# Row-tiled pairs for half of the Q projection, and another order of the K stage, in a block of linear attention plus GEGLU on one Trainium2 core

## Chip, cores and metric

The kernel runs on one core of one Trainium2 chip. The metric is the device time of one execution in microseconds (us). Lower is better. All matrices are bf16, with sums in f32.

The engines are named as in the profile: PE is TensorE's matmul, PEld its weight load, DVE is VectorE, ACT is ScalarE, POOL is GpSimd, SP is SyncE (here it only issues transfers and hands on signals). Each engine works through its own instructions in the order in which the program issues them.

## What is computed

```python
def _A_ref(x, wqkv, wo):                      # x: 1 x 2048 x 576, 32 heads of 18
    q, k, v = split_heads(x @ wqkv)
    phi = lambda t: jnp.where(t > 0, t + 1, jnp.exp(t)) + 1e-6
    pq, pk = phi(q), phi(k)
    kv = jnp.einsum("bhsd,bhse->bhde", pk, v)
    z = jnp.einsum("bhsd->bhd", pk)
    num = jnp.einsum("bhqd,bhde->bhqe", pq, kv)
    den = jnp.einsum("bhqd,bhd->bhq", pq, z)[..., None] + 1e-6
    return merge_heads(num / den) @ wo

def _B_ref(x, w_gate, w_up, w_down):          # inner size 4608
    return (_gelu(x @ w_gate) * (x @ w_up)) @ w_down

xn = _layernorm(A_x)
return A_x + _A_ref(xn, A_wqkv, A_wo) + _B_ref(xn, B_w_gate, B_w_up, B_w_down)
```

## The kernel before

The 2048 tokens are 16 tiles of 128 (`NS`) or 4 slices of 512 (`NSC`). The 576 features are 4 full tiles of 128 rows and one of 64; in the normalized input `xn` the last 64 columns are stored twice, so its fifth tile also has 128 rows. The 32 heads are 5 chunks (`NCH`): four of 7 heads (126 rows) and one of 4 (72 rows). PSUM is one tensor `ps_all` of 8 banks of 512 f32.

**K stage** (16 token tiles). For a tile n: DVE takes statistics of two halves and aggregates them (`ln_half`, L200 and L202); ACT makes 1/sqrt by Ln and Exp (`ln_rstd`, L206, L207); DVE normalizes (`ln_norm`, L210); POOL stores the last 64 columns a second time (`ln_dup`, L216); PE transposes five tiles into bank 7 (`transposes`, L222); ACT copies them to `xnT` (`tp_copy`, L226); PE makes K in two halves of 288 columns, banks 5 and 6 (`k_half`, L234); ACT reads each half with relu (L251), DVE with max (L255), ACT takes one exp over both (L262), and POOL adds the two into `pk` (L266). DVE's read of a bank waits for ACT's read of it.

V is never made. In its place PE sums the Gram matrix of `xn` and `pk` over the tokens (`g_accumulate`, L281): part `G_A` in the K stage in banks 0 to 4, two tiles behind K (`GLAG`), ten matmuls a tile; the remainder `G_B`, two matmuls a tile, later in banks 0 and 1, once `G_A` has been copied to `g_sb` (`g_copy`, L428).

The order of the K stage is a timetable: `STEPS` (L387) gives each step of a tile a time for tiles 0 to 4 and then a step of 2.5 (`TILE`) per tile; all steps of all tiles are sorted by that time and issued in this order. All transfers up to the first four gate/up blocks are issued ahead of it (L413 to L420).

**Q part** (20 units: 4 slices by 5 chunks, `q_unit`). A unit is five matmuls with 512 columns (L306), then phi: mostly relu and exp on ACT, max on DVE and an add on POOL; every third unit one exp on ACT and two steps on DVE. The intermediate tiles are `phi_e` (three buffers) and `phi_a` (two). Units 0 and 1 are in the timetable, units 2 to 19 in the loop at L431, which also carries: the last two tiles of `G_A`, the copies of `g_sb`, the z product (`z_stage`, L343, masked into `zrep`), the remainder `G_B` in units 6 to 13, the denominators of slice 0 in units 13 to 17 (`den_mm`, L366, evicted by ACT), and the product of `wv` and the Gram matrix (`kv_stage`, L354, masked into `kvT`) at unit 17.

**Gate/up and down**, once for each slice. `gu_pair` takes blocks of two units; a unit is a gate and an up product of 128 inner columns. These run in row tiles: the array is used as two halves of 64 rows that work at the same time, LO and HI, on different banks (`_Unit`). In the first half `p1` the gate product takes the LO rows and the up product the HI rows, ten matmuls; in the second half `p2` they change sides, eight matmuls, and a signal that goes from PE to SP and back (`turn`, L488) keeps one bank from being written by both. The second halves follow the first halves of the next unit. Then comes gelu on ACT (L522) and the product on DVE (L523), while the denominators of slice 0 are inverted on DVE and multiplied on POOL (`den_norm`). The down product (L550) and the attention's output (L555) follow. The first load of `w_down` (L461) waits until the buffers of the attention part have been read.

Of the kernel before, what the change touches and what calls it, by code (L numbers as in the profile page):

```python
# [15 lines left out]
P = 128  # L16
# [23 lines left out]
GLAG = 2  # L40
XW = 642
# [14 lines left out]
def kernel(  # L56
# [45 lines left out]

    def load_w(which):
        c = slice(which * D, (which + 1) * D)
        nc.sync.dma_start(wqkv_sb[:, 0:4, c], A_wqkv[0:512, c].rearrange("(kt p) c -> p kt c", p=P))
        nc.sync.dma_start(wqkv_sb[0:HP, 4, c], A_wqkv[512:576, c])

# [89 lines left out]
    def ln_half(n, a_):  # L197
        if a_ == 0:
            stats_t[n] = asmall.tile([P, 2, nc.vector.BN_STATS_DIM], F32, name="stats")
        nc.vector.bn_stats(out=stats_t[n][:, a_, :], in_=x_sb[:, n, a_ * HALF:(a_ + 1) * HALF])  # L200
        if a_ == 1:
            nc.vector.bn_aggr(out=mv[:, n, :], in_=stats_t.pop(n)[:])  # L202

    def ln_rstd(n):
        r = rstd[:, n:n + 1]
        nc.scalar.activation(out=r, in_=mv[:, n, 1:2], func=ACT.Ln, bias=eps_ln[:], scale=1.0)  # L206
        nc.scalar.activation(out=r, in_=r, func=ACT.Exp, scale=-0.5)  # L207

    def ln_norm(n):
        nc.vector.tensor_scalar(  # L210
            out=xn[:, n, 0:D], in0=x_sb[:, n, :], scalar1=mv[:, n, 0:1], scalar2=rstd[:, n:n + 1],
            op0=ALU.subtract, op1=ALU.mult,
        )

    def ln_dup(n):
        (nc.gpsimd if n else nc.vector).tensor_copy(out=xn[:, n, D:640], in_=xn[:, n, 512:D])  # L216
# [7 lines left out]
    def tp_copy(n):  # L224
        copy = acopy if n else vcopy
        copy(out=xnT[:, :, n * P:(n + 1) * P], in_=tp_bank[:, 0:KT, :])  # L226
# [20 lines left out]
    def k_relu(n, hf):  # L247
        if hf == 0:
            k_ea[n] = phi_tiles()
        hs = slice(hf * HALF, (hf + 1) * HALF)  # L250
        nc.scalar.activation(out=k_ea[n][0][:, hs], in_=ps_all[:, k_bank(n, hf), :HALF], func=ACT.Relu, scale=-1.0)  # L251

    def k_max(n, hf):
        hs = slice(hf * HALF, (hf + 1) * HALF)
        nc.vector.tensor_scalar(  # L255
            out=k_ea[n][1][:, hs], in0=ps_all[:, k_bank(n, hf), :HALF],
            scalar1=0.0, scalar2=EPS_ATT, op0=ALU.max, op1=ALU.add,
        )

    def k_exp(n):  # L260
        e = k_ea[n][0]
        nc.scalar.activation(out=e[:], in_=e[:], func=ACT.Exp, scale=-1.0)  # L262

    def k_add(n):
        e, a = k_ea.pop(n)
        nc.gpsimd.tensor_tensor(out=pk[:, n, :], in0=e[:], in1=a[:], op=ALU.add)  # L266
# [10 lines left out]
    def g_accumulate(n, pieces):  # L277
# [7 lines left out]

    vcopy, acopy = nc.vector.tensor_copy, nc.scalar.copy

    G_COPIES = {
        4: [(0, G_A, 0, acopy), (0, G_A, 1, vcopy), (2, G_A, 0, acopy), (2, G_A, 1, vcopy)],
# [4 lines left out]
    }  # L294

# [3 lines left out]
    def q_unit(i):  # L299
# [3 lines left out]
        cs = slice(sc * SC, (sc + 1) * SC)  # L303
        ps = ps_all[:rows, q_banks.next(), :]
        for kt in range(KT):
            nc.tensor.matmul(  # L306
                ps, lhsT=wqkv_sb[:, kt, q0:q0 + rows], rhs=xnT[:, kt, cs],
                start=(kt == 0), stop=(kt == KT - 1),
            )
        e, a = phi_tiles()  # L310
# [63 lines left out]
    def den_norm(sc, c, q, pieces):  # L374
# [8 lines left out]

    TILE = 2.5
    STEPS = [  # L387
        (lambda n: ln_half(n, 0), [3.02, 3.99, 6.44, 7.41, 9.44]),
        (lambda n: ln_half(n, 1), [3.51, 4.48, 6.93, 7.90, 9.93]),
        (ln_rstd, [4.14, 5.11, 7.56, 10.12, 11.84]),  # L390
        (ln_norm, [4.96, 5.69, 8.38, 10.77, 12.80]),
        (ln_dup, [5.43, 6.16, 8.85, 11.24, 13.27]),
        (transposes, [5.66, 6.57, 9.14, 11.53, 13.62]),
        (tp_copy, [6.07, 6.98, 9.56, 12.27, 14.12]),
        (lambda n: k_half(n, 0), [6.86, 8.09, 10.30, 13.01, 15.56]),
        (lambda n: k_half(n, 1), [7.47, 9.43, 10.91, 13.91, 16.46]),
        (lambda n: k_relu(n, 0), [7.99, 9.28, 11.56, 13.84, 16.55]),
        (lambda n: k_relu(n, 1), [8.27, 10.55, 12.83, 15.11, 17.39]),
        (lambda n: k_max(n, 0), [8.72, 10.41, 12.44, 14.61, 17.27]),
        (lambda n: k_max(n, 1), [9.08, 11.11, 13.28, 15.60, 17.84]),  # L400
        (k_exp, [8.73, 11.12, 13.29, 15.61, 18.10]),
        (k_add, [9.59, 11.73, 14.01, 16.29, 19.88]),
    ]
    G_AT = [11.82, 14.53, 17.07, 19.62, 22.16]

    def at(times, n):
        return times[n] if n < len(times) else times[-1] + TILE * (n - len(times) + 1)

    todo = [(at(times, n), step, n) for n in range(NS) for step, times in STEPS]
    todo += [(at(G_AT, n), lambda n: g_accumulate(n, G_A), n) for n in range(NS - GLAG)]  # L410

    todo += [(at(STEPS[7][1], NS - 1) - 0.01, q_unit, 0), (at(G_AT, NS - GLAG) - 0.01, q_unit, 1)]
    load_x(8, 4)  # L413
    load_x(12, 4)
    load_w(0)
    load_w(2)
    load_wo()
    for i in range(NWBUF):
        load_gu(i, 0)
        load_gu(i, 1)  # L420
    for _, step, n in sorted(todo, key=lambda x: x[0]):
        step(n)
# [8 lines left out]
    for i in range(2, NSC * NCH):  # L431
# [3 lines left out]
        if 3 <= i < 3 + GLAG:  # L435
            g_accumulate(NS - GLAG + i - 3, G_A)
        for kt, pieces, part, copy in G_COPIES.get(i, ()):
            g_copy(kt, pieces, part, copy)
        if i == 10:
            z_stage()  # L440
        if 6 <= i < 14:
            for n in (2 * (i - 6), 2 * (i - 6) + 1):
                g_accumulate(n, G_B)
        if 13 <= i < 13 + NCH:
            den_mm(0, i - 13, q_banks.next())
        if i == 17:
            kv_stage()
# [16 lines left out]

    LO, HI = slice(0, HP), slice(HP, P)
    SYNC = mybir.DependencyInfo(mybir.DependencyClass.Sync, mybir.DependencyReason.DATA)
    banks = _Ring(list(range(8)))  # L470

    class _Unit:


        def __init__(self, outs, lhs, rhs):
            self.outs, self.lhs, self.rhs = outs, lhs, rhs

        def mm(self, i, rows, kt, start, stop):
            return nc.tensor.matmul(  # L479
                self.outs[i], lhsT=self.lhs(i, rows, kt), rhs=self.rhs(i, rows, kt),  # L480
                start=start, stop=stop, skip_group_check=True,
            )

        def p1(self):
            for kt in (4, 0, 1, 2, 3):
                self.mm(0, LO, kt, kt == 4, False)
                last = self.mm(1, HI, kt, kt == 4, False)
            self.turn = nc.sync.nop()  # L488
            tc.add_manual_dep(self.turn.ins, last.ins.name, SYNC, reason="the row tiles take turns on a bank")

        def p2(self):
            for kt in range(4):
                m = self.mm(1, LO, kt, False, kt == 3)
                if kt == 0:
                    tc.add_manual_dep(m.ins, self.turn.ins.name, SYNC, reason="the bank's other row tile has written")
                self.mm(0, HI, kt, False, kt == 3)
# [28 lines left out]
    m_banks = _Ring(list(range(2, 8)))  # L525
# [85 lines left out]
```

## Time and profile before

| | us |
|---|---|
| median of 5 runs | 531.38 |
| lowest, highest | 530.52, 531.57 |
| the profiled execution | 531.57 |
| its span | 529.8 |
| first transposes on PE | 5.50 |
| first Gram step on PE | 12.79 |
| first Q unit on PE | 43.96 |
| first gate/up matmul | 76.94 |
| first gelu | 80.18 |

The span runs from the first to the last recorded instruction; a time of an execution holds 1.77 us more. Times in the timeline are from the start of the span. The shares of busy time are averages over stages: up to 44 us the K stage, to 77 us the Q part, then four rounds of gate/up and down. The granted clock of TensorE is full in all 40 slices.

In a line of the timeline stand the start, the length, the engine, the line of the code, the operation, what it writes and reads, and how many instructions were merged; in brackets the idle time before and what ended it. Matmuls are pipelined: one that follows another starts before the other's recorded end.

### The profile page before, as it was taken

Reading aid. Unit: us, or ns where it says so; the run is one execution under the profiler, and the core shown is the slowest. Engines: PE = TensorE matmul, PEld = TensorE weight load, DVE = VectorE, ACT = ScalarE, POOL = GpSimd, SP = SyncE. Lnnn points to the kernel's source line nnn. Section 1 sums busy time; section 2 is a strip of 40 time slices with the busy share of each in tenths; the row PEclk is TensorE's granted clock in tenths of the full one; section 3 lists DMA queues with packets and bytes.
Section 4 is the critical chain, followed back from the end, with each engine's and each line's share of the span. In section 5 each row is a group of like instructions: output and inputs, shape, how many; then the busy total and the mean of one; then the engine's idle time right before and its main releaser. Section 6 shows DMA issues by size and latency. Waiting matters only on the chain.

```text
span 529.8 us, 10752 instructions
## 1 busy us (share of the span) xinstructions
PE 521.6 (98%) x4532; PEld 311.6 (59%) x4532; DVE 246.9 (47%) x408; ACT 153.7 (29%) x296; POOL 70.3 (13%) x83
## 2 busy tenths in 40 slices
PE   7999999999999999999999999999999999999997
PEld 6887664444477754444477744444677544445775
DVE  7884767773348513333368233333585143333101
ACT  6997693323230013323200022323100132322000
POOL 3666552110002100000012000000021000000000
PEclk9999999999999999999999999999999999999999
DMA  8910006999510025555400055555100355540000
GB/s 269 263 30 1 1 2 198 263 265 260 149 31 20 16 80 152 148 149 157 136 12 12 12 151 162 148 157 156 47 22 12 95 145 158 155 135 1 12 12 22
DMA packets 98810, 55.85 MB, mean 105 GB/s; under 512 B 5322, under 2 KB 98378, under 8 KB 98762
## 3 DMA queue, kind: packets, MB, share of 16 engines
q1 hardware_dynamic: 98762, 55.17, 36.2%
q8 instruction: 35, 0.57, 0.4%
q14 instruction: 13, 0.11, 0.1%
HBM read 52.79 MB, written 2.36 MB: 104 GB/s over the span
## 4 chain that ended last, share of the span: by engine, by line
PE 93%; SPq 3%; DMA 1%; DVE 1%; issue 1%; POOL 0%; ACT 0%; DVEq 0%; POOLq 0%; ACTq 0%
PE ps_all L479 50%; PE ps_all L550 27%; PE ps_all L306 4%; PE ps_all L555 4%; PE ps_all L281 3%; PE ps_all L234 3%; DMA x_sb<-in_A_x_dram 1%; SPq L165 1%; PE ps_all L366 1%; PE ps_all L222 1%; SPq L167 1%; SPq L168 1%; SPq L92 0%; DVE phi_a L255 0%; DVE stats L200 0%
## 5 line engine op out<-in xcount | busy, mean ns | idle before, releaser
L479 PE MATMUL ps_all<-xnT,wu 64*128 64x512 bf16 x1152 | 273.2, 376 | 1.1 <-SPq L488 0.5
L479 PE MATMUL ps_all<-xnT,wg 64*128 64x512 bf16 x1152 | 273.6, 376 | 0.0
L523 DVE TENSOR_TENSOR hT<-ps_all,gl 128x512 bf16<-128x512 f32 x144 | 99.6, 692 | 169.2 <-ACT gl L522 169.0
L522 ACT ACTIVATE gl<-ps_all 128x512 f32<-128x512 f32 x144 | 86.0, 597 | 316.8 <-PE ps_all L479 295.0
L479 PEld LDWEIGHTS <-wu 64*128 64x128 bf16 x1152 | 107.2, 94 | 72.3 <-SPq L488 8.7
L479 PEld LDWEIGHTS <-wg 64*128 64x128 bf16 x1152 | 107.2, 94 | 67.9
L550 PE MATMUL ps_all<-wd_sb,hT 128*128 128x288 bf16 x1152 | 146.5, 286 | 0.0
L550 PEld LDWEIGHTS <-hT 128*128 128x128 bf16 x1152 | 112.3, 98 | 31.4 <-issue 1.9
L380 DVE RECIPROCAL den_sb<-den_sb 126x128 f32<-126x128 f32 (+1 forms) x80 | 68.3, 911 | 0.5
L381 POOL TENSOR_TENSOR pqT<-pqT,den_sb 126x512 bf16<-126x512 bf16 (+3 forms) x25 | 24.1, 965 | 302.1 <-DVE den_sb L380 298.8
L558 DVE TENSOR_TENSOR res<-ps_all,x_sb 128x288 bf16<-128x288 f32 x32 | 14.6, 458 | 88.3 <-PE ps_all L555 88.3
L479 PE MATMUL ps_all<-xnT,wr 64*128 64x512 bf16 x288 | 54.7, 376 | 0.0
L555 PE MATMUL ps_all<-m_sb,pqT 126*128 126x288 bf16 (+1 forms) x160 | 24.9, 285 | 0.0
L234 PE MATMUL ps_all<-wqkv_sb,xnT 128*128 128x288 bf16 x160 | 24.3, 286 | 0.4 <-ACT xnT L226 0.2
L306 PE MATMUL ps_all<-xnT,wqkv_sb 128*126 128x512 bf16 (+1 forms) x100 | 24.4, 380 | 0.1
L479 PEld LDWEIGHTS <-wr 64*128 64x128 bf16 x288 | 14.0, 94 | 17.7 <-issue 1.1
L281 PE MATMUL ps_all<-hT,xn 128*128 128x288 bf16 (+3 forms) x192 | 23.6, 266 | 0.0
L266 POOL TENSOR_TENSOR hT<-phi_e,phi_a 128x576 bf16<-128x576 f32 x16 | 22.5, 1406 | 4.6 <-ACT phi_e L262 3.6
L281 PEld LDWEIGHTS <-xn 128*128 128x128 bf16 (+1 forms) x192 | 18.1, 101 | 4.6 <-issue 0.3
L316 POOL TENSOR_TENSOR pqT<-phi_e,phi_a 126x512 bf16<-126x512 f32 (+1 forms) x14 | 17.6, 1268 | 16.2 <-DVE phi_a L314 11.3
L555 PEld LDWEIGHTS <-pqT 126*128 126x128 bf16 (+1 forms) x160 | 15.5, 97 | 4.1
L255 DVE TENSOR_SCALAR phi_a<-ps_all 128x288 f32<-128x288 f32 x32 | 14.3, 451 | 7.1 <-ACT phi_e L251 5.6
(58 smaller groups left out, 202.8 us busy)
## 6 DMA issues: line engine op xcount, KB each, us to landing
wg<-in_B_w_gate_dram SPq DMA_DIRECT2D x72, 256.0 KB, 2.8
wu<-in_B_w_up_dram SPq DMA_DIRECT2D x72, 256.0 KB, 3.3
wd_sb<-in_B_w_down_dram SPq DMA_DIRECT2D x12, 432.0 KB, 4.5
wr<-in_B_w_gate_dram SPq DMA_DIRECT2D x72, 32.0 KB, 2.6
wr<-in_B_w_up_dram SPq DMA_DIRECT2D x72, 32.0 KB, 3.0
out_dram<-res SPq DMA_DIRECT2D x15, 144.0 KB, 1.8
x_sb<-in_A_x_dram SPq DMA_DIRECT2D x3, 576.0 KB, 7.6
wqkv_sb<-in_A_wqkv_dram SPq DMA_DIRECT2D x2, 576.0 KB, 9.9
```

The source lines that it names most:

```text
L234: nc.tensor.matmul(ps_all[:, k_bank(n, hf), :HALF], lhsT=xnT[:, kt, n * P:(n + 1) * P], rhs=wqkv_sb[:, kt, D + hf * HALF:D + (hf + 1) * HALF],
L266: nc.gpsimd.tensor_tensor(out=pk[:, n, :], in0=e[:], in1=a[:], op=ALU.add)
L281: nc.tensor.matmul(ps_all[:m, b, col:col + w], lhsT=xn[:, n, j0:j0 + m], rhs=pk[:, n, d0:d0 + w], start=(n == 0 and col == 0), stop=(n == ...
L306: nc.tensor.matmul(ps, lhsT=wqkv_sb[:, kt, q0:q0 + rows], rhs=xnT[:, kt, cs], start=(kt == 0), stop=(kt == KT - 1),)
L316: nc.gpsimd.tensor_tensor(out=pqT[:rows, c, cs], in0=e, in1=a, op=ALU.add)
L380: nc.vector.reciprocal(out=d[:, h:h + P], in_=d[:, h:h + P])
L381: nc.gpsimd.tensor_tensor(out=pqT[:rows, c, cols], in0=pqT[:rows, c, cols], in1=d, op=ALU.mult)
L479: return nc.tensor.matmul(self.outs[i], lhsT=self.lhs(i, rows, kt), rhs=self.rhs(i, rows, kt), start=start, stop=stop, skip_group_check=True,)
L522: nc.scalar.activation(out=gl[:], in_=ps_all[:, b[0], :], func=ACT.Gelu_apprx_tanh)
L523: nc.vector.tensor_tensor(out=hT[:, GUB * k + i, :], in0=ps_all[:, b[1], :], in1=gl[:], op=ALU.mult)
L550: nc.tensor.matmul(acc, lhsT=hT[:, f, j * P:(j + 1) * P], rhs=wd_sb[:, f, hs], start=(f == 0), stop=False,)
L555: nc.tensor.matmul(acc, lhsT=pqT[:rows, c, ts_], rhs=m_sb[:rows, c, hs], start=False, stop=(c == NCH - 1),)
```

## The change

The second half of the Q projection (slices 2 and 3, ten units) is computed in five pairs with `_Unit`, the row-tiled scheme of gate/up, directly ahead of gate/up. For that `_Unit` is moved up in the file unchanged, Q's last 64 weight rows are loaded a second time into rows 64 to 127 (`wq_lo`), and `q_unit` is split into matmuls and phi (`q_phi`). Units 2 to 9 stay as they were, in the loop; the Gram remainder is put into units 5 to 9, the z product to unit 8, and the denominators of slice 0 and `kv_stage` stand between unit 9 and the pairs. The rings of banks are changed to fit.

The timetable is gone: the K stage is a loop over the tiles with a fixed order, with the first tiles written out. From tile 7 on the rstd of two tiles is made by one pair of ACT instructions. The calls that load x, Wq, Wv, Wo and the first gate/up blocks stand inside the loop; the order of the transfers on SP is as before, with the one load of `wq_lo` added.

```diff
     def load_w(which):
...
+        if which == 0:
+            nc.sync.dma_start(wq_lo[HP:P, :], A_wqkv[512:576, c])
...
-    TILE = 2.5
-    STEPS = [
-        (lambda n: ln_half(n, 0), [3.02, 3.99, 6.44, 7.41, 9.44]),
...
-    for _, step, n in sorted(todo, key=lambda x: x[0]):
-        step(n)
+    ln_stats(2)
+    ln_rstd(0)
+    ln_stats(3)
+    ln_norm(0, nc.vector)
+    transposes(0)
+    ln_stats(4)
+    tp_copy(0, 0, KT, vcopy)
+    ln_rstd(1)
+    k_half(0, 0)
+    ln_norm(1)
+    transposes(1)
+    ln_stats(6)
+    k_half(0, 1)
+    k_read(0, 0)
+    tp_all(1)
+    ln_rstd(2)
+    ln_stats(7)
+    k_half(1, 0)
+    ln_norm(2)
+    k_read(0, 1)
+    k_finish(0)
+    transposes(2)
+    k_half(1, 1)
+    ln_stats(9)
+    for n in range(1, NS):
+        if n > 1:
+            k_half(n, 0)
+            k_half(n, 1)
+        if n + 1 < NS:
+            tp_all(n + 1)
+        if n + 2 < NS and (n + 2 < PAIRED or n % 2 == 1):
+            ln_rstd(n + 2, min(1 if n + 2 < PAIRED else 2, NS - n - 2))
+        if n + 2 < NS:
+            ln_norm(n + 2)
+        k_read(n, 0)
+        k_read(n, 1)
+        k_finish(n)
+        ln_stats(2 * (n + 4) + (1 if n < PAIRED - 4 else 2))
+        if n >= GLAG:
+            g_accumulate(n - GLAG, G_A)
+        if n + 2 < NS:
+            transposes(n + 2)
+        if n in (NS - 2, NS - 1):
+            q_unit(q_next[0])
+            q_next[0] += 1
...
+    G_B_AT = {4: (), 5: (0, 1), 6: (2, 3, 4), 7: (5, 6, 7), 8: (8, 9, 10, 11), 9: (12, 13, 14, 15)}
...
-    for i in range(2, NSC * NCH):
+    for i in range(2, 2 * NCH):
         if i == 8:
             q_banks = _Ring([2, 3, 4, 5, 6, 7])
         q_unit(i)
-        if 3 <= i < 3 + GLAG:
-            g_accumulate(NS - GLAG + i - 3, G_A)
+        if i < 2 + GLAG:
+            g_accumulate(NS - GLAG + i - 2, G_A)
         for kt, pieces, part, copy in G_COPIES.get(i, ()):
             g_copy(kt, pieces, part, copy)
-        if i == 10:
+        if i >= 4:
+            for n in G_B_AT[i]:
+                g_accumulate(n, G_B)
+        if i == 8:
             z_stage()
...
+    for kt, pieces, part, copy in G_COPIES[14]:
+        g_copy(kt, pieces, part, copy)
+    for c in range(NCH):
+        den_mm(0, c, q_banks.next())
+    kv_stage()
+
+    q_banks = _Ring([7, 0, 1, 2, 3, 4, 5, 6])
+    prev = None
+    for k, items in enumerate([[(2, 0), (2, 1)], [(2, 2), (2, 3)], [(2, 4), (3, 4)], [(3, 0), (3, 1)], [(3, 2), (3, 3)], None]):
+        if items:
+            u = q_pair(items)
+            u.p1()
+        if prev:
+            prev[1].p2()
+            for i, (sc, c) in enumerate(prev[0]):
+                q_phi(2 * k + i, sc, c, prev[1].outs[i])
+        prev = (items, u)
```

The new functions that this calls:

```python
def ln_stats(halves):                  # statistics up to this many halves of tiles
    while ln_done[0] < min(halves, 2 * NS):
        n, a_ = divmod(ln_done[0], 2)
        ...
        ln_done[0] += 1

def ln_norm(n, dup=None):              # now with the copy of the last 64 columns
    ...
    (dup or nc.gpsimd).tensor_copy(out=xn[:, n, D:640], in_=xn[:, n, 512:D])

def k_read(n, hf):                     # relu on ACT, max on DVE
def k_finish(n):                       # exp on ACT, add on POOL
def tp_all(n):
    tp_copy(n, 0, KT, acopy)

def q_pair(items):
    rows = DH * HCH[items[0][1]]
    b = [q_banks.next(), q_banks.next()]
    outs = [ps_all[:rows, b_, :] for b_ in b]

    def lhs(i, r, kt):
        q0 = DH * HOFF[items[i][1]]
        if kt == 4 and r.start:
            return wq_lo[r, q0:q0 + rows]
        return wqkv_sb[r, kt, q0:q0 + rows]

    return _Unit(outs, lhs, lambda i, r, kt: xnT[r, kt, items[i][0] * SC:(items[i][0] + 1) * SC])
```

## The prediction

> **What bounds the kernel now.** I read the engines' busy shares first, then the chain of work that ended last, then the timeline of TensorE.
>
> ```profile
> PE 521.6 (98%) x4532; PEld 311.6 (59%) x4532; DVE 246.9 (47%) x408; ACT 153.7 (29%) x296; POOL 70.3 (13%) x83
> PE   7999999999999999999999999999999999999997
> PE 93%; SPq 3%; DMA 1%; DVE 1%; issue 1%; POOL 0%; ACT 0%; DVEq 0%; POOLq 0%; ACTq 0%
> L306 PEld LDWEIGHTS <-wqkv_sb 128*126 128x126 bf16 x80 | 10.5, 136 | 5.3 <-issue 0.4
> ```
>
> TensorE is the bound from end to end, so a change counts only as matmul time removed or as gaps opened or closed on TensorE. Busy time hides gaps (records overlap), so I count start to start. One token tile of the K stage, from the timeline at 24 us:
>
> ```profile
> 24.05 0.78 PE L234 MATMUL ps_all<-wqkv_sb,xnT 128*128 128x288 bf16 x5
> 24.66 0.44 PE L222 MATMUL ps_all<-ident,xn 128*128 128x128 bf16 x5
> 24.94 0.78 PE L234 MATMUL ps_all<-wqkv_sb,xnT 128*128 128x288 bf16 x5
> 25.55 1.15 PE L281 MATMUL ps_all<-hT,xn 128*128 128x288 bf16 x10
> 26.54 0.78 PE L234 MATMUL ps_all<-wqkv_sb,xnT 128*128 128x288 bf16 x5
> ```
>
> K half 0.61, transposes 0.28, K half 0.61, Gram 0.99: 2.49 us a tile, each starting where the last one's columns end. TensorE is full here; no order makes it faster. The Q part and its end, from the timeline of TensorE:
>
> ```profile
> 47.27 3.72 PE L306 MATMUL ps_all<-xnT,wqkv_sb 128*126 128x512 bf16 x15
> 50.82 1.15 PE L281 MATMUL ps_all<-hT,xn 128*128 128x288 bf16 x10
> 51.81 1.24 PE L306 MATMUL ps_all<-xnT,wqkv_sb 128*72 128x512 bf16 x5
> 53.03 1.15 PE L281 MATMUL ps_all<-hT,xn 128*128 128x288 bf16 x10
> 77.17 0.38 PE L479 MATMUL ps_all<-xnT,wg 64*128 64x512 bf16 x1
> 77.17 0.38 PE L479 MATMUL ps_all<-xnT,wu 64*128 64x512 bf16 x1
> 77.17 0.09 PEld L479 LDWEIGHTS <-wg 64*128 64x128 bf16 x1
> 77.17 0.09 PEld L479 LDWEIGHTS <-wu 64*128 64x128 bf16 x1
> 77.38 0.38 PE L479 MATMUL ps_all<-xnT,wg 64*128 64x512 bf16 x1
> ```
>
> A slot of 512 columns is 0.2155 us (77.17 to 77.38, and over many). Two 64-row matmuls share a slot. A plain Q unit is five slots, 1.078. The first row shows three units, 3.23, and takes 3.55: a gap of 0.32; the third, five slots, takes 1.22: a gap of 0.14.
>
> **The change, part by part.** Sums are made against the profiled execution: span 529.8, time 531.57, so 1.77 lies around the span; the median of the five is 531.38, 0.19 less.
>
> *Pairs.* Ten Q units leave (50 slots) and five pairs of nine slots come (45): 5 x 0.2155 = -1.08 us. The switch into row tiles (last plain matmul starts about 76.62, first row-tiled 76.94: 0.32 instead of 0.22) is there before too; it only moves ahead of the pairs. The wait between the halves goes over SP; between first half k and its second half lie 4 or 9 slots (0.86 or 1.94 us) of another pair, the same 4 as in gate/up, where matmuls lost 0.5 us to that line in 144 units: nothing. Weights of 126 columns load in 136 ns (L306) against 94 for 128 in 64 rows (L479); both tiles load at the same moment and 136 is under 215: nothing; if the two loads ran one after the other, 0.272 a slot, 45 x 0.057 = +2.5. I take nothing, because the rows at 77.17 show both loads and both matmuls starting together.
>
> The Trainium skill, TensorE: Matmul & The Clock Gate (Part 3, what overlaps and what doesn't), says that a weight load overlaps running matmuls only in another row group, which would forbid this. By it a slot would be 0.2155 + 0.136 and the pairs would cost some 6 us more (an estimate); the rows at 77.17 deny it, since slots stay 0.2155 with the next weights loading under the running matmul of the same rows.
>
> *Gaps of the Q part.* The 0.32 is the third Q unit waiting for bank 5 until the K max of tile 15 has read it (max at 48.16, matmul at 48.67). That max waited 1.45 for POOL's add of Q unit 0, as phi_a has two buffers and unit 0's steps were issued ahead of tile 14's add. In the new order tile 14's and 15's reads come first and Q unit 1 (1.08) stands between: K half at t, relu t+1.4, max t+1.85 to 2.3, while bank 5 is wanted at t+3.3 (two K halves 1.22, Gram 0.99, one unit 1.08). The 0.14 is a Gram step waiting for tile 15's add, which also comes earlier. I follow the rest on TensorE: Gram remainder needs copies two units earlier, banks free by then; the z product comes 1 unit after its copies; masks end about 0.2 before the first denominator; kv's last chunk needs the bank of denominator 0 and has 20 short matmuls in front. Nothing opens: -0.46. Bounds: 0 (gaps only move) and -0.55 (all gaps from 42.98 to 76.94: 33.96 less 33.41 of work).
>
> *K stage.* Same instructions, except that from tile 7 two tiles share one rstd pair (0.31 + 0.20 saved on ACT per two tiles, off the path). The order is new and every engine runs in order, so I played it by hand with the rows' durations, start to start where one follows another. Start of the Gram steps, before then after: G0 12.79, 13.22; G1 15.60, 15.71; G2 18.09, 18.20; G3 20.57, 20.70; G4 23.06, 23.47. Where they come from: the x transfer of tiles 4 to 7 lands at 10.65 in both; the first statistics half of tile 4 now stands ahead of norm 3 on DVE, so norm 3 starts 11.22 and transposes 3 at 11.65; TensorE has these ahead of K of tile 2, which before ran at 10.96 and now starts 12.0. Norm 4 (13.64) is then early enough and most is caught up. At tile 5 the rstd of 7 and 8 waits for the second tile's aggregate (DVE 20.56, after two tiles' statistics); norm 7 21.42, transposes 21.87 with TensorE free at 21.69, its last one held by POOL's copy to 22.17: +0.41 and it stays.
>
> From there the longest loop over two tiles is: aggregate to norm 0.85 (0.24 + 0.33 + 0.28), norm to the last transpose 0.74 (0.45 to POOL's copy, 0.24, 0.05), to K 0.08, half to half 0.61, to relu 0.86, to max 0.47, to statistics 0.37, to aggregate 0.86: 4.84 against TensorE's 4.98. TensorE stays the bound by 0.14. So +0.43; from below 0 (G1 to G3 show how much is caught up), from above the loop with full durations in place of spacings (rstd 0.65, norms 0.78, four max 1.80, statistics 1.0 and 1.0): 5.23, or +0.25 for each of some 5.5 pairs of tiles, +1.4 more.
>
> *SP.* The order of transfers is unchanged, the calls only move in the program; one 72 KB load is added behind Q's weights. A like one (L106) held SP 1.1 to 2.2 us, so the loads behind it (V, Wo, first gate/up blocks) are that much later: the last issues at 25.59 before, wanted from 73 on. Nothing; that cover is 45 us deep.
>
> *Denominators and kv first, pairs last.* The ten evictions now crowd at the end: six with relu, exp on ACT (0.60 + 0.63), max (0.69) and POOL's add (1.27), four with one exp (0.60) and two DVE steps (0.69 + 0.78); ACT alone has 9.8 us for 9.7 of pairs, after five denominators of 0.67. From the pairs' start P the first is read at P+3.25; phi_a's two buffers and POOL's adds then pace it; the last max step ends P+14.9, ACT's last exp P+13.8, the table load (1.28) P+15. Gate/up's fourth unit wants bank 0 at P+9.70+3.88+1.08 = P+14.66: +0.24. The first gelu is 2 us late, but its banks are wanted again only at P+17.5, after mult at P+16.4. Wd's first load waits for these buffers until P+15.6; before it went out at 83.39, 6.45 after gate/up's start, which is P+16.1 here: nothing. Bounds 0 and +1 (POOL's add one step later).
>
> The skill's TensorEngine Tiling (PSUM Bottleneck) says that row tiling speeds TensorE and not eviction; ACT's 9.8 against 9.7 agrees, and by it alone the gain would vanish; eight banks of lag are why I charge only 0.24.
>
> Sum: -1.08 - 0.46 + 0.43 + 0.24 = -0.87. Span 528.9, time 530.7 for an execution like the profiled one, 530.5 for the median.
>
> **Rivals.** *The statistics loop sets the K stage's pace.* It is slower than before from 5.14 per two tiles on (0.87 / 5.5 over 4.98), and by 0.2% from 5.33. For it: the margin is 0.14 in eleven hand-offs. Against: on DVE a next step starts 0.30 to 0.37 after one of 0.39 to 0.45. At 5.23 it gives 530.5 + 1.4 = 531.9; with POOL's copy also held by the 1.41 add (0.35 once in my walk) 5.58, 533.8. *Weight loads of the two tiles in turn:* 530.5 + 2.5 = 533.0; against it the rows at 77.17, for it only the longer load. *All lateness is absorbed:* no start loss in K and no wait at bank 0 gives -1.54, 529.8; for it the catching up at G1; against it the rstd of two tiles.
>
> **How the numbers follow.** Forecast 0.50, loop 0.24, loads in turn 0.08, absorbed 0.18. Runs of this kernel tell 0.2% (1.06 us) from no change. The forecast's own range is 529.9 to 531.1, of which four tenths lie under 530.32: faster 0.20 + 0.18 = 0.38; same 0.30 and half the loop's 0.24: 0.42; slower 0.12 + 0.08 = 0.20. Range 529.6 to 532.6: it holds the forecast, the absorbed case and the lighter half of the loop.
>
> **What would show it.** Right: Gram steps 2.49 apart from tile 5 on, G4 0.3 to 0.5 late; no gap between the last K tile and the pairs; slots of 0.2155 in the pairs, five pairs in 9.7; first gelu late by some 2 us with TensorE waiting under 0.5. Wrong: Gram steps 2.55 or more apart with transposes waiting for norm or POOL's copy; slots of 0.27 in the pairs; a wait over 1 us at the first gate/up units.

## The result, and the profile after

The changed kernel takes 532.69 us (median of 34 runs, 531.58 to 533.97) where the kernel before, run beside it, takes 531.24 (57 runs, 529.71 to 532.95): a ratio of 1.0027, with a 95% interval of 1.0021 to 1.0033. It is slower by 1.45 us. The forecast was 530.5 with a range up to 532.6, so the time lies just outside it and on the other side of no change. The profiled execution after takes 532.68 with a span of 531.0, 1.2 more than the span of 529.8 before.

The page of the changed kernel, the lines that were read first of the kernel before (busy time of each engine; TensorE in 40 slices of the span, in tenths; and the shares of the chain of waits that ended last):

```profile
PE 522.2 (98%) x4572; PEld 326.5 (61%) x4572; DVE 250.0 (47%) x409; ACT 151.7 (29%) x287; POOL 69.0 (13%) x82
PE   7999999999999999999999999999999999999997
PE 91%; SPq 3%; ACT 2%; DVE 1%; issue 1%; POOL 1%; DMA 0%; POOLq 0%; ACTq 0%
```

TensorE is still busy for 98% of the span. But its share of the chain of waits has gone from 93 to 91%, and ACT and POOL, 0% before, now have 2 and 1%: some of the work ends by other engines' pace. Start times on TensorE say where (us from the span's start, or length of a stage):

| | before | after |
|---|---|---|
| first Gram step (tile 0) | 12.79 | 13.17 |
| Gram step of tile 4 | 23.06 | 23.45 |
| Gram step of tile 12 | 42.98 | 44.19 |
| first pair | | 66.87 |
| first gate/up matmul | 76.94 | 76.63 |
| four gate/up rounds | 72.10, 71.82, 70.34, 70.35 | 72.68, 71.45, 71.19, 70.81 |

Up to gate/up the change has won 0.31 us. The four rounds of gate/up, whose instructions are the same ones (on other banks), then give back 0.58 - 0.37 + 0.85 + 0.46 = 1.52. The sum, +1.21, is the difference of the spans but for 0.1. The loss therefore has three places: the K stage (1.21 lost where 0.43 was forecast), the first round of gate/up, and the later rounds. The middle is as forecast: from the Gram step of tile 12 to gate/up 33.96 before, 32.44 after, -1.52.

Of the 1.21 in the K stage 0.38 is there at the first Gram step already. That start differs from one execution to the next: in the three other runs below that keep the K stage of the kernel before it stands at 12.53, 13.45 and 13.46, in those with the new order at 13.15 to 13.58. No run shows that the change moved it. From the first Gram step to that of tile 12 there is no such spread: 30.19 before (30.11 to 30.18 in the three others), 31.02 after (30.93 and 30.99 in the two others with the loop unchanged). So 0.83 is what the order of the loop costs.

The loop of the K stage, from the timeline of the changed kernel (start, length, engine, line, operation; in brackets the idle time before and its end):

```profile
25.99 1.15 PE L285 MATMUL ps_all<-hT,xn 128*128 128x288 bf16 x10
...
26.64 0.43 DVE L222 TENSOR_SCALAR xn<-x_sb,mv,rstd 128x576 bf16<-128x576 bf16 x1 [0.60 <-ACT rstd L219]
...
28.00 1.41 POOL L270 TENSOR_TENSOR hT<-phi_e,phi_a 128x576 bf16<-128x576 f32 x1 [0.63 <-ACT phi_e L269]
...
28.72 0.86 DVE L222 TENSOR_SCALAR xn<-x_sb,mv,rstd 128x576 bf16<-128x576 bf16 x1
28.74 1.15 PE L285 MATMUL ps_all<-hT,xn 128*128 128x288 bf16 x10
...
31.23 1.15 PE L285 MATMUL ps_all<-hT,xn 128*128 128x288 bf16 x10
...
32.37 0.53 PE L232 MATMUL ps_all<-ident,xn 128*128 128x128 bf16 x5
...
33.23 1.41 POOL L270 TENSOR_TENSOR hT<-phi_e,phi_a 128x576 bf16<-128x576 f32 x1 [0.62 <-ACT phi_e L269]
...
33.95 0.85 DVE L222 TENSOR_SCALAR xn<-x_sb,mv,rstd 128x576 bf16<-128x576 bf16 x1
33.98 1.15 PE L285 MATMUL ps_all<-hT,xn 128*128 128x288 bf16 x10
```

The Gram steps stand at 25.99, 28.74, 31.23, 33.98: 2.75 and 2.49 in turn, 5.24 for two tiles where it was 4.98. The two norms (L222) are the same instruction on the same shape, and one takes 0.43, the other 0.86. Neither the bracket nor any list of waits shows a cause: an instruction that is held up after its start (called held from here on) looks like a long one. What differs is POOL: its add (L270) runs from 28.00 to 29.41 and the long norm ends at 29.58; the next add runs from 33.23 to 34.64 and the long norm ends at 34.80. The two short norms (26.64, and 31.88 in the next pair of tiles) lie outside of any add. Over the 16 norms the mean goes from 400 ns before to 559 after. Behind the held norm on DVE stand the max of the K tile and the next statistics, and so the next rstd and the transposes (the 0.53 at 32.37, which hold TensorE, in place of 0.28 of pure work).

The start of the pairs, the start of gate/up and its fourth unit, timeline of the changed kernel:

```profile
66.87 0.43 PE L321 MATMUL ps_all<-xnT,wqkv_sb 64*126 64x512 bf16 x1
...
76.63 0.38 PE L321 MATMUL ps_all<-xnT,wr 64*128 64x512 bf16 x2
...
80.58 2.50 POOL L378 TENSOR_TENSOR pqT<-phi_e,phi_a 126x512 bf16<-126x512 f32 x2 [1.30 <-ACT phi_e L377]
...
81.60 0.38 PE L321 MATMUL ps_all<-xnT,wr 64*128 64x512 bf16 x1
81.89 0.69 DVE L382 TENSOR_SCALAR phi_a<-ps_all 126x512 f32<-126x512 f32 x1 [0.85 <-POOL pqT L378]
82.37 1.09 ACT L586 ACTIVATE gl<-ps_all 128x512 f32<-128x512 f32 x2
82.61 1.02 DVE L383 SCALAR_TENSOR_TENSOR pqT<-phi_e,phi_a 126x512 bf16<-126x512 f32 x1
82.63 0.37 PE L321 MATMUL ps_all<-xnT,wr 64*128 64x512 bf16 x1 [0.66 <-DVE phi_a L382]
```

A unit is a gate and an up product, one on each half of the array at a time. One half starts its fourth unit at 81.60; the other half's first matmul of this unit, which belongs at the same time, comes at 82.63. That is 1.03 of idle time on the one half, and 0.82 on the other, which can go on no sooner than that. The bracket names the last step that reads bank 0 (L382 at 81.89), and that step waited for POOL, which had to free phi_a.

The later rounds, from the list of waits on TensorE, first of the kernel before and then of the changed one (in total, times, longest):

```profile
PE ps_all L479 <- SPq L488: 0.5, 3, 0.2
```

```profile
PE ps_all L321 <- SPq L330: 0.8, 5, 0.2
PE ps_all L321 <- DVE phi_a L382: 0.7, 1, 0.7
```

This is the signal that goes from PE over SP and back between the halves of a unit. The list counts only time in which no record is open on TensorE; start to start the gaps above 30 ns in the four rounds sum to 2.74 before (0.43, 1.71, 0.29, 0.30) and to 4.22 after (1.01, 1.36, 1.11, 0.74), of which 0.8 to 1.0 is the fourth unit's. One of them, SP and TensorE in the timeline of the kernel before:

```profile
195.34 0.38 SPq L164 DMA_DIRECT2D wg<-in_B_w_gate_dram  x1
...
195.77 1.47 SPq L165 DMA_DIRECT2D wr<-in_B_w_gate_dram  x1
...
197.36 0.52 SPq L167 DMA_DIRECT2D wu<-in_B_w_up_dram  x1
...
197.92 0.51 SPq L168 DMA_DIRECT2D wr<-in_B_w_up_dram  x1
...
198.55 0.39 PE L479 MATMUL ps_all<-xnT,wu 64*128 64x512 bf16 x1 [0.15 <-SPq L488]
```

SP issues transfers and hands on the signal in one order. The issue at 195.77 occupies it for 1.47 us, so the two issues of the block's second unit come late (197.36 and 197.92). That unit's signal stands behind them, and its second half starts at 198.55, 0.32 late.

### The profile page after: what moved, and what is told of

It reads as the page before. It is cut to its first block, busy times and chain, and to the rows that moved or that the text cites. A ratio compares the mean times of both kernels' runs of the same rounds, so it can differ in the third digit from the quotient of the medians.

```text
span 531.0 us, 10832 instructions
## 1 busy us (share of the span) xinstructions
PE 522.2 (98%) x4572; PEld 326.5 (61%) x4572; DVE 250.0 (47%) x409; ACT 151.7 (29%) x287; POOL 69.0 (13%) x82
## 4 chain that ended last, share of the span: by engine, by line
PE 91%; SPq 3%; ACT 2%; DVE 1%; issue 1%; POOL 1%; DMA 0%; POOLq 0%; ACTq 0%
PE ps_all L321 50%; PE ps_all L614 27%; PE ps_all L619 4%; PE ps_all L285 4%; PE ps_all L243 3%; PE ps_all L349 2%; SPq L171 1%; PE ps_all L232 1%; PE ps_all L428 1%; POOL pqT L378 1%; SPq L173 1%; SPq L174 1%; DMA x_sb<-in_A_x_dram 0%; DVE stats L211 0%; ACT phi_e L377 0%
## 5 line engine op out<-in xcount | busy, mean ns | idle before, releaser
L321 PE MATMUL ps_all<-xnT,wg 64*128 64x512 bf16 x1152 | 274.7, 376 | 0.0
L321 PE MATMUL ps_all<-xnT,wu 64*128 64x512 bf16 x1152 | 272.4, 376 | 1.4 <-SPq L330 0.8
L321 PEld LDWEIGHTS <-wu 64*128 64x128 bf16 x1152 | 106.8, 94 | 66.2 <-SPq L330 9.6
L321 PEld LDWEIGHTS <-wg 64*128 64x128 bf16 x1152 | 106.9, 94 | 62.2 <-issue 1.2
L321 PE MATMUL ps_all<-xnT,wr 64*128 64x512 bf16 x288 | 57.1, 376 | 0.7 <-DVE phi_a L382 0.7
L321 PEld LDWEIGHTS <-wr 64*128 64x128 bf16 x288 | 15.9, 94 | 15.7 <-issue 0.7
L270 POOL TENSOR_TENSOR hT<-phi_e,phi_a 128x576 bf16<-128x576 f32 x16 | 22.5, 1404 | 9.0 <-DVE phi_a L263 4.7
L243 PE MATMUL ps_all<-wqkv_sb,xnT 128*128 128x288 bf16 x160 | 22.6, 286 | 0.6 <-DVE xnT L235 0.6
L378 POOL TENSOR_TENSOR pqT<-phi_e,phi_a 126x512 bf16<-126x512 f32 (+1 forms) x13 | 16.4, 1269 | 18.3 <-DVE phi_a L376 11.4
L243 PEld LDWEIGHTS <-xnT 128*128 128x128 bf16 x160 | 15.0, 98 | 4.6 <-DVE xnT L235 0.9
```

Of the source, the lines that this page charges most:

```text
L243: nc.tensor.matmul(ps_all[:, k_bank(n, hf), :HALF], lhsT=xnT[:, kt, n * P:(n + 1) * P], rhs=wqkv_sb[:, kt, D + hf * HALF:D + (hf + 1) * HALF],
L321: return nc.tensor.matmul(self.outs[i], lhsT=self.lhs(i, rows, kt), rhs=self.rhs(i, rows, kt), start=start, stop=stop, skip_group_check=True,)
L378: nc.gpsimd.tensor_tensor(out=pqT[:rows, c, cs], in0=e, in1=a, op=ALU.add)
```

## The experiments

They ask three things: what holds the norm, what makes the fourth unit wait, and how much of the time is the signal's. Each time is a median with its lowest and highest run, and each ratio is against the kernel before as run on the same chip.

**The old timetable with the pairs.** The changed kernel with the K stage issued as before; the Q part and the pairs stay.

```diff
-    for n in range(1, NS):
...
+    STEPS = [
...
+    for _, step, n in sorted(todo, key=lambda x: x[0]):
+        step(n)
```

> The changed kernel with the K stage of before (timetable, one rstd per tile) put back; pairs and everything behind the K stage stay. Theory A (the K stage lost 1.2 us because the second norm of each pair of tiles runs into POOL's add): Gram steps 2.49 apart throughout, thirteenth Gram step back at 43.0 from 44.2, the gap of 0.3 at the third Q unit returns, so some 0.9 us less than the changed kernel: 531.8. Theory B (the loss lies behind the K stage, at the pairs and gate/up): no less than the changed kernel, 532.7.

Measured: 532.95 (531.53 to 534.87), ratio 1.0037 [1.0023, 1.0052]. No gain. The Gram step of tile 12 is at 42.70, 1.49 earlier than in the changed kernel (0.64 of it is the earlier first Gram step, at 12.53), but gate/up starts at 76.65, as there. The timeline shows where it is given back:

```profile
46.57 1.26 POOL L371 TENSOR_TENSOR pqT<-phi_e,phi_a 126x512 bf16<-126x512 f32 x1 [3.07 <-DVE phi_a L369]
...
51.30 1.40 POOL L272 TENSOR_TENSOR hT<-phi_e,phi_a 128x576 bf16<-128x576 f32 x1
...
52.75 1.15 PE L287 MATMUL ps_all<-hT,xn 128*128 128x288 bf16 x10 [1.05 <-POOL hT L272]
```

The timetable issues the steps of Q unit 0 ahead of tile 14's add; POOL's Q add at 46.57 comes first, and the Gram steps of the last two tiles wait for POOL (1.05 at 52.75). The two orders belong together: here the old K order doesn't go with the new filling behind it. So this run doesn't separate the K stage from the rest, and its expectation was missed.

**The second norm issued earlier.** If the norm is held by POOL's add, the same instructions in another place cost nothing. In each pair of tiles the second norm is issued a turn earlier, ahead of the statistics.

```diff
-        if n + 2 < NS:
+        if n + 2 < NS and (n + 2 < PAIRED or n % 2 == 1):
             ln_norm(n + 2)
         k_read(n, 0)
         k_read(n, 1)
         k_finish(n)
+        if n + 3 < NS and n + 3 > PAIRED and n % 2 == 1:
+            ln_norm(n + 3)
```

> The changed kernel with one edit: from tile 8 on the second tile's norm of each rstd pair is issued ahead of the statistics, in the same turn as the first, so that it starts before POOL's add does. Same instructions. Theory A (a norm that starts while POOL's add runs is held until the add has ended, 0.83 to 0.86 in place of 0.38 to 0.43): the moved norms take 0.38 to 0.45, two tiles take 4.98 to 5.05 in place of 5.24, thirteenth Gram step at 43.3 to 43.5, 0.7 to 0.9 us less than the changed kernel. Rival (DVE's steps simply do not overlap, 5.23 as in the second case of the prediction): two tiles stay at 5.2, no change.

Measured: 531.53 (530.89 to 533.47), ratio 1.0012 [1.0003, 1.0022], where the changed kernel has 1.0027. Its timeline:

```profile
27.54 0.42 DVE L222 TENSOR_SCALAR xn<-x_sb,mv,rstd 128x576 bf16<-128x576 bf16 x1
27.79 1.43 POOL L270 TENSOR_TENSOR hT<-phi_e,phi_a 128x576 bf16<-128x576 f32 x1 [0.62 <-ACT phi_e L269]
...
28.65 1.15 PE L285 MATMUL ps_all<-hT,xn 128*128 128x288 bf16 x10
...
31.14 1.15 PE L285 MATMUL ps_all<-hT,xn 128*128 128x288 bf16 x10
```

The norm now starts ahead of the add and takes 0.42; the Gram steps are 2.49 apart from tile 4 on, and from the first to that of tile 12 it is 30.18 again. Gate/up starts at 76.03, 0.60 earlier than in the changed kernel, although the first Gram step came 0.24 later. No instruction was removed from the program. So the 5.24 comes from where the second norm stands, under POOL's add, and the rival falls by which the durations of the loop's steps add up to it in any order.

**One rstd for each tile.** The same question from the other side, in a single run: the pairing of the rstd is undone, and the loop is otherwise the changed one.

```diff
-        if n + 2 < NS and (n + 2 < PAIRED or n % 2 == 1):
-            ln_rstd(n + 2, min(1 if n + 2 < PAIRED else 2, NS - n - 2))
+        if n + 2 < NS:
+            ln_rstd(n + 2)
```

> The changed kernel with one rstd per tile throughout (no pairs of tiles). Theory A: every norm then comes at the same place in a tile's 2.49, as in tiles 3 to 6 of the changed kernel where it meets only the end of POOL's add (0.52 to 0.56): Gram steps 2.49 to 2.53 apart, thirteenth at 43.1 to 43.6. Rival (ACT, with 0.25 more per tile, becomes the bound): 2.6 or more apart.

Measured: 530.34, beside 531.64 for the kernel before (a single time, so its size is not to be relied on); Gram steps 2.49 apart from tile 4 on, gate/up at 75.53. The norms still meet POOL's add in part, and from tile 7 on their durations fall from 670 to 438 ns as the overlap falls from 504 to 268; the duration follows the overlap, tile by tile. Without the pairing the hold is there but has room. So it is the pairing of the rstd, two instructions saved on an engine with time to spare, that puts the second norm under the add and DVE's queue behind it.

**A third phi_a buffer.** For the fourth unit: with three buffers the step that reads bank 0 needn't wait for POOL's add.

```diff
-        a = awork.tile([P, D], F32, name="phi_a", tag="phi_a", bufs=2)
+        a = awork.tile([P, D], F32, name="phi_a", tag="phi_a", bufs=3)
```

> The changed kernel with three buffers of phi_a in place of two. Theory A (the evictions of the pairs are paced by POOL's adds through two buffers, and the scalar_tensor_tensor steps are held by the adds): the waits of 0.84 of DVE for POOL go, the last max-like step ends 1 to 2 us earlier, the gap of 0.82 to 1.03 on TensorE at 81.6 goes and the first gate/up round takes 70.2 to 70.6 in place of 71.07: 0.5 to 0.8 us less than the changed kernel. Rival (the gap is an offset between the two row tiles or SP's signal, not the buffers): gap stays, no change.

Measured: 531.83 (530.79 to 533.15), ratio 1.0014 [1.0004, 1.0025], where the changed kernel has 1.0027. The timeline at the same place:

```profile
80.48 2.50 POOL L378 TENSOR_TENSOR pqT<-phi_e,phi_a 126x512 bf16<-126x512 f32 x2 [1.30 <-ACT phi_e L377]
...
80.99 0.69 DVE L382 TENSOR_SCALAR phi_a<-ps_all 126x512 f32<-126x512 f32 x1
...
81.49 0.62 PE L321 MATMUL ps_all<-xnT,wr 64*128 64x512 bf16 x2
81.72 1.81 DVE L383 SCALAR_TENSOR_TENSOR pqT<-phi_e,phi_a 126x512 bf16<-126x512 f32 x1
```

The read of bank 0 starts at 80.99 and waits for nothing, and the wait at the fourth unit falls from 0.82 and 1.03 to 0.04 and 0.25. The step after it (L383) is held by POOL longer than before, 1.81 against 1.02, which now costs nothing, since the bank is free by then.

**The loads issued behind the signals.** For the later rounds: in a block of two gate/up units the transfers are issued after both first halves, so that no signal of the block stands behind them on SP. This edit in the kernel before, and the same in the changed kernel:

```diff
-            if blk > 0:
-                load_gu(blk + NWBUF - 1, i)
             u.p1()
             units.append((b, u))
+        if blk > 0:
+            for i in range(GUB):
+                load_gu(blk + NWBUF - 1, i)
```

> The kernel before with one edit in gate/up: the loads of a later block are issued on SP behind the two signals of a block, not between them. Theory C (the gate/up rounds of 70.3 to 71.8 us hold single gaps of 0.3 on TensorE because a signal over SP stands behind two transfer issues): rounds of 69.9 to 70.1, gaps of 0.3 gone, some 2 us less than before, 529.3. Rival (the gaps come from the landing of the weights): no change or longer, as the loads go out 2 us later.

> The changed kernel with the same edit in gate/up as in the kernel before with late loads (529.49): loads behind the two signals. With the signal's waits gone from both, what is left between the two is the change itself. Theory D (the change itself costs what its trace shows: gate/up starts 0.3 earlier, then a wait of 0.8 to 1.0 at the fourth unit): 530.0 to 530.4, which is 0.5 to 0.9 over 529.49; so of the 1.4 lost in the result some 0.7 is waiting for the signal that falls out worse. Rival (all 1.4 belong to the change's own places): 530.9. Rounds 2 to 4 take 69.7 from first to last matmul in either case.

Measured: the kernel before with it takes 529.49 (528.66 to 529.91), ratio 0.9969 [0.9957, 0.998]; the changed kernel with it 530.39 (529.71 to 531.43), ratio 0.9974 [0.9961, 0.9986]. Rounds 2 to 4 take 70.04 to 70.07 in both and have no gap. The late loads bring the kernel before 1.66 us by the medians on the same chip (531.15 to 529.49), and the changed one 2.8 by the ratios (1.0027 to 0.9974). So some 1.2 of the 1.45 that the change lost would be more waiting for the same signal, in code that it didn't touch, and what stays, 0.3 (0.9974 against 0.9969), the change's own cost. The intervals allow about 0.9 either way, so that both sizes are rough. The profiles of the result give the same own cost: 0.83 in the loop of the K stage, 1.52 won from there to gate/up, and 1.03 lost at the fourth unit, +0.34 in all. But they show only some 0.5 more of waiting for the signal, and the runs with the moved norm and with the third buffer, whose gate/up code is the changed kernel's, lose 2.2 in rounds 2 to 4 against 70.04 each, where the changed kernel loses 3.3 and the kernel before 2.4. How much more the changed kernel waits for the signal in general is therefore not shown.

**A load more on SP.** Does the added load of `wq_lo` shift the transfers and so the waits? The kernel before with that load, which nothing reads.

```diff
+    wq_lo = apool.tile([P, D], BF16, name="wq_lo")
...
+        if which == 0:
+            nc.sync.dma_start(wq_lo[HP:P, :], A_wqkv[512:576, c])
```

> The kernel before with the one 72 KB load of Wq's last rows added and not used. Theory G (the changed kernel waits 0.6 more for signals because one more transfer shifts every later transfer among the slots that they wait for): 0.4 to 0.8 more than before. Rival (the extra load does nothing): no change within 0.3.

Measured: 530.69 (530.43 to 532.71), ratio 0.9999 [0.9988, 1.001]. It isn't the load. If the changed kernel does wait more for the signal, why stays open; the gaps differ from one execution to another, and one profile of each shows only one of them.

**All three mends, with the pairs and without.** The changed kernel with the norm moved, the third buffer and the late loads; and the same with ten plain units in place of the five pairs:

```diff
-    prev = None
-    for k, items in enumerate([[(2, 0), (2, 1)], [(2, 2), (2, 3)], [(2, 4), (3, 4)], [(3, 0), (3, 1)], [(3, 2), (3, 3)], None]):
...
+    for i in range(2 * NCH, NSC * NCH):
+        q_unit(i)
```

> The changed kernel with the norm moved, three buffers of phi_a and the late loads together. If the three costs are separate they add up: gate/up starts at 75.9 to 76.1, a wait of at most 0.3 at the fourth unit, rounds of 69.7 to 70.0: 528.3 to 528.8, faster than both kernels and than the kernel before with late loads. Rival (what the pairs gain is always given back at the fourth unit): not below 529.4.

> As the run with all three, but the ten units of the second half are plain units in the same place and with the same banks. Measures the pairs alone. Theory E: five slots of 0.2155 come back, gate/up starts 1.1 later and the evictions have 1.1 more time, so the wait at the fourth unit is 0: 0.8 to 1.1 us more than the run with all three. Rival (evictions decide, not matmuls): same time.

Measured: with pairs 529.02 (528.08 to 529.61), ratio 0.9951 [0.9935, 0.9967]; without them 528.85 (528.71 to 529.03), ratio 0.9947 [0.9931, 0.9962]. Both take 0.5% less than the kernel before. But the pairs bring nothing, where 0.8 to 1.1 us was expected. They were run again beside each other:

> The run with all three again, beside the next on one chip. Theory E: 0.3 to 0.9 less than without pairs, the gate/up start 1.1 earlier less what is waited at the fourth unit. Rival: level.

> The run without pairs again. Theory E: 0.3 to 0.9 more than the run with all three. Rival: level. Spread of its runs under 0.5, as no signal is waited for.

Measured: 528.95 (528.54 to 529.24), ratio 0.9963 [0.9951, 0.9975], and 529.01 (528.74 to 529.96), ratio 0.9968 [0.9955, 0.9981]. The two are level again. And these ratios are close to that of the kernel before with the late loads alone (0.9969), so that no gain of the rest is clear either. On TensorE the pairs are won: gate/up starts at 75.75 and 75.88 with them, at 77.05 and 77.06 without. But the second round of gate/up starts at 190.55 in the second run with pairs and at 190.63 and 190.65 without (189.81 in the first profile with pairs, that kernel's fastest run). In the second run with pairs the whole 1.2 is lost within the first round, in the first one some 0.5 of it. The second run with pairs, SP and TensorE in the timeline, some 26 us into that round:

```profile
99.42 1.27 SPq L173 DMA_DIRECT2D wu<-in_B_w_up_dram  x1
...
100.74 0.52 SPq L174 DMA_DIRECT2D wr<-in_B_w_up_dram  x1
...
101.30 0.59 SPq L560 DMA_DIRECT2D wd_sb<-in_B_w_down_dram  x1
...
102.00 0.39 PE L321 MATMUL ps_all<-xnT,wu 64*128 64x512 bf16 x1 [0.24 <-SPq L330]
```

In the first round SP has five transfers in a block, `w_down` being the fifth; an issue that takes 1.27 pushes the others back, and the next block's signal behind them: 0.57 and 0.41 of gap on the two halves here, 0.35 some 38 us into the round, 0.24 at the fourth unit. Without pairs the first round has at most 0.03 of gaps, though SP has issues of 1.0 to 1.4 there too.

**The two-step units first.** A last try to keep the gain: with all three mends, each pair but the last evicts a unit by the two DVE steps first, which moves these steps off the end.

```diff
-                q_phi(2 * k + i, sc, c, prev[1].outs[i])
+                q_phi(2 if i == 0 and k < 5 else 0, sc, c, prev[1].outs[i])
```

> The run with all three, and in the pairs the units with two DVE steps and no POOL add are the first of the pairs one to four, so that the last pair has none; same count of four. Theory F (what is left of the wait at the fourth unit is the last pair's max step behind a two-step unit that POOL's add holds 1.8): the gap of 0.23 at the fourth unit goes, first round 69.8 to 70.0 from first to last matmul, and the pairs then keep most of their 1.08: 0.5 to 1.0 less than the run without pairs. Rival (the pairs' gain is taken back by whatever follows): level with the run without pairs.

Measured: 528.64 (528.37 to 528.89), ratio 0.9959 [0.9947, 0.997], the lowest median of all, though within 0.4 of the others. The wait at the fourth unit is gone, and the first round has other gaps in its place: 0.58 and 0.39 some 14 us into it, with 1.58 us for one issue of SP ahead. The second round starts at 190.61, as without pairs.

So in four of five profiles the second round starts at 190.55 to 190.65, whether gate/up began at 75.88, 76.13 or 77.06. That looks as if something else paced the first round, but the fifth, 189.81, shows that it is no fixed floor. The traces show SP's long issues, and 240 to 270 GB/s with the DMA engines 83 to 91% busy from 85 to 132 us in the second run with pairs; whether one of the two sets a pace wasn't tried and stays open.

## Why the prediction was wrong

The forecast was -0.87; between the two profiles it is +1.21. Of the 2.08 that lie between them 0.78 are the K stage's, 0.79 the fourth unit's, and 0.49 waits in the rounds of gate/up that the prediction put at nothing; the part from the K stage to gate/up is off by 0.02.

**Pairs, -1.08: right on TensorE, of no worth at the end.** Five pairs take 9.76 us, forecast 9.70; slots are 0.2155, so the weight loads of 126 columns (133 ns in 64 rows) hide under running matmuls, and the rival of loads in turn falls. What the prediction left out is that the next stage must be able to use an earlier start. By the runs with and without pairs nothing of it was left at the end.

**Gaps of the Q part, -0.46: right.** With the pairs, -1.54 was forecast from the last K tile to gate/up and -1.52 came.

**K stage, +0.43: the step that failed.** The hand walk had the spacing of the first tiles right: from the first Gram step the next four come 2.51, 5.00, 7.52 and 10.28 later, forecast 2.49, 4.98, 7.48 and 10.25. That the times themselves agree too (13.17 against 13.22) is luck: the walk has the transfer of x for tile 4 landing at 10.65, in this execution tile 4's statistics start at 10.23, and the first Gram step moves by more than the +0.43 between executions of one order. From the first Gram step to that of tile 4 the kernel before takes 10.27, so that no run shows the +0.43 as the change's. Then came the claim that a loop of 4.84 leaves TensorE the bound "by 0.14". Measured is 5.24 for two tiles, and 0.83 lost from the first Gram step to tile 12. The loop was put together from spacings, the shortest times at which one step can follow another, in which the second norm of a pair isn't there, and it took DVE's durations to be fixed. With POOL's add at the same time the norm's is not: the 4.84 and the 0.43 of the hold make 5.27 (an estimate), close to the 5.24. The rival "statistics loop" has the right size, 5.23, by another mechanism, full durations in place of spacings; the moved norm shows that with the same instructions in place the pace is 4.98. A number that agrees doesn't confirm its reason.

The row that told of it was in the timeline of before:

```profile
12.88 1.41 POOL L266 TENSOR_TENSOR hT<-phi_e,phi_a 128x576 bf16<-128x576 f32 x1 [0.21 <-ACT rstd L206]
...
13.96 0.50 DVE L210 TENSOR_SCALAR xn<-x_sb,mv,rstd 128x576 bf16<-128x576 bf16 x1
```

One of the 16 norms, at 13.96, took 498 ns where the other 15 took 377 to 432; it was the one that overlapped POOL's add, and it ended 0.17 after the add's end. The second step of the two-step unit at 52.38 was another such row (L321, 1151 ns in place of 692, ended 0.55 after the add). The Trainium skill, SBUF — State Buffer (Who interferes with whom), states the rule: "Whoever issues first gets the shared pair for the whole instruction; the other fully blocks", for a DVE instruction in a two-port mode, or with two inputs from SBUF, against a GpSimd instruction that reads SBUF. The runs agree: held norms end 0.17 after POOL's add, held steps of L383 0.55 after it, while the max from PSUM (450 ns) and the statistics keep their times under the add. In the run with the moved norm the norm starts first: it keeps its 0.42, and the adds that it overlaps by 0.17 to 0.19 take 1.43 to 1.46 in place of 1.40, longer, but by less than the overlap. It is the rule that should have been weighed against this change; which mode the norm runs in, no row here shows.

**Fourth unit, +0.24: right mechanism, wrong size.** 0.82 and 1.03 came. Two steps of L383 ahead of it (at 75.03 and 78.81) were held by 0.33 each, and the last max step then waited 0.85 for POOL to free phi_a: it ended 15.71 after the pairs' start in place of 14.9. That the wait is phi_a's and POOL's the third buffer shows. The prediction's bound of +1 just about held it.

**Signal over SP: "nothing", the second step that failed.** The 0.5 us of the list of waits was taken for its price. The list counts only time without an open record; start to start, the gaps are 2.74, and taking the transfers out of the signal's way brings 1.66 in the kernel before. What was mispriced there was a cost of both kernels; in the changed one it is larger by 0.5 in the two profiles and by some 1.2 by the ratios, and the cause of that stays open.

**First gelu and `w_down`, nothing.** The gelu came 2.2 late (82.37 against 80.18), and no wait of TensorE names it. The first load of `w_down` left at 84.09 (83.39 in the kernel before): 7.46 after gate/up's start in place of 6.45, and no matmul waits for `w_down`. But its loads share SP with the signals of the first round, which wasn't counted.

## What to carry to other kernels

When a step is moved, ask which instructions of DVE and POOL it puts side by side, and look in the trace for one operation with two durations: here that was a hold, and no list of waits named it. Time won ahead of a stage counts only if the stage can start and run earlier, so test the stage's start and its end. A signal that shares a queue with transfers can be late by the issues ahead of it; here its place within a block was worth 0.3% in a kernel with nothing else changed. And compare stages from a mark inside the kernel (here the first Gram step): the start itself moved by 0.9 us between executions with the same K stage.

## What the runs showed that was not expected

- A norm of 128x576 bf16 takes 0.38 to 0.43 us alone and up to 0.86 under POOL's add of 1.4; a two-input step of 126x512 takes 0.69 alone and up to 1.82 under POOL's adds. A max of 128x288 from PSUM takes 0.45 either way.
- The issue of one and the same kind of load (`wr`, 32 KB, of the gate) occupies SP for 0.50 to 1.49 us in the kernel before, from gate/up on.
- Without most of the signal's waits the runs lie somewhat closer: a standard deviation of 0.38 us over the ten runs without pairs (528.71 to 529.96), 0.68 over the 57 of the kernel before. The first five alone (528.71 to 529.03) looked closer than the second five.
